# A fused transformer block on one core: key tile in three blocks, value tile with its own history, and a new written-out order

## The chip, the core and the metric

The kernel runs on one core of a Trainium2 chip. A core has five engines with their own instruction streams: TensorE (PE in the profile; its weight loads are listed apart as PEld), VectorE (DVE), ScalarE (ACT), GpSimd (POOL) and SyncE (SP). SP issues nearly all transfers here; they run on the core's 16 DMA engines. The engines meet only through semaphores: an instruction waits until what it reads has been written. Each engine works through its own list in the order in which the program issued it, so an instruction that waits holds up everything behind it on its engine. The metric is the time of one execution in microseconds (us); it was measured three times for the kernel before.

## The reference

One block of a transformer on x of 2048 rows by 512, in bf16. A vector c gives, through SiLU and w_mod, six vectors of 512: shift, scale and gate for each half.

```
mod = silu(c) @ w_mod                      # six vectors sa, ca, ga, sb, cb, gb
h = layernorm(x) * (1 + ca) + sa
q, k, v = h @ wqkv                         # 32 heads of 16
# position s looks at s, s-2, ..., s-14 (8 places, none before 0)
attn = softmax(q[s] . k[s - 2w] / 4 over w)
x = x + ga * ((sum over w of attn * v[s - 2w]) @ wo)
h = layernorm(x) * (1 + cb) + sb
x = x + gb * ((gelu(h @ w_gate) * (h @ w_up)) @ w_down)
```

The hidden width of the last part is 1792.

## The kernel before, in words

The rows are worked on in four groups of 512 (`sg` 0 to 3). A group passes through these steps, each a Python generator that yields `Op` objects; an `Op` has an engine, the names that must be done before (`after`), buffer slots that it takes and gives, and a function that issues the instructions.

- Norm 1 (`LN1.sg`): statistics on DVE (`st0` to `st3`, line 430; one or more of the four are done on ACT, `sa` and `sq`, lines 408 and 419), then the reciprocal root on POOL (`rs0`, line 471), then the scaling on DVE (`x0` to `x3`, line 448) into the tile xn. POOL's `rs0` reads what DVE wrote (`vd0`, `va0`, lines 460 and 465), and `x0` reads what POOL wrote.
- Turning the normed rows (`transp`): for group 0 and 1 by TensorE (`LN1.0.th`, line 509; `LN1.1.t0`, `t1`, line 484), for groups 2 and 3 by a transposing transfer that SP issues (`LN1.2.t`, `LN1.3.t`, line 490).
- Scale and shift (`h0` to `h3`, one for each 128 columns): group 0 on DVE and ACT out of PSUM, groups 1 and 3 on ACT (line 527), group 2 on POOL (line 525). They write hT, which the projection reads.
- Projection (`qp.sg.blk.j`, four matmuls of 512 columns each, line 598): blk 0 is q, 1 is k, 2 is v; j is one of four sets of heads. A matmul of index dt reads h of the same index. ACT empties PSUM (`qkv.sg.blk.j`).
- Logits: DVE multiplies q with eight shifted views of k (`pq.sg.j`, line 664, one instruction of 128x4096), TensorE sums with a small matrix in 32-column tiles (`lp`, line 678, eight matmuls that run four at a time).
- Softmax on DVE, with the exponential on ACT (`mx`, `z`, `e`, `s1`, `ri`, `p`), then the weights are turned (`ptp` on TensorE for group 0, a write to DRAM and four reads, `est` and `ptl`, for groups 1 to 3).
- Values: v goes to DRAM (`vst`, line 635) and comes back in four reads, each for 32 partitions and shifted by two rows against the next (`V4.sg.0` to `V4.sg.2` and `V4ld.sg`, line 644). DVE multiplies (`pv.sg.j`, line 771), TensorE sums (`o.sg.j`, line 790).
- Output projection (`x1p`), the addition of x (`x1`), norm 2 (`LN2.sg`), then the gated part: 14 pairs of `g` and `u` (line 844), `gl` and `ub` on ACT, their product `hh` on DVE, the down projection `y` (line 856), the last addition `ot` and the store `sto`.

Gates: the vector ga is made on TensorE (`mp2`), copied (`gc2`), written to DRAM (`gst2`, line 319) and read back to all partitions (`ga`, line 323), where it scales wo (`woS`). The same is done for gb (`mp5`, `gst5`, `gb`).

What runs when is fixed by one list of numbers, `ORDER`: each number names a generator, and its next `Op` is issued. There is no planner at run time, and nothing reorders. The list fixes the order of each engine:

```
for i in ORDER:
    op = nxt[i]
    ...
    op.fn()
```

K lies in one tile with room for three groups and 16 columns of history in front (`kT`, line 170); the view of group sg starts 14 columns before its first. When group 3 writes over group 0, a copy (`halo`, line 630) brings the last columns of group 2 to the front. V has one tile for a group (`v4`, one buffer) that holds the group's 512 positions and 8 before them, so each read fetches rows of 520 elements. A mask tile serves the first positions of group 0.

Of the kernel before, what the change touches and what calls it, by code (L numbers as in the profile page):

```python
# [106 lines left out]
def kernel(  # L107
# [23 lines left out]
    VH = 16  # L131
    VR = S + VH

# [5 lines left out]
    NB = {"x": 4, "hT": 2, "xn": 2, "q": 4, "vs": 1, "v4": 1, "prod": 5, "h2": 2,  # L139
# [17 lines left out]
    maskT = const.tile([H, W, 16], F32, name="maskT")  # L157
# [12 lines left out]
    kT = const.tile([P, 4, 3 * SG + 16], BF16, name="kT")  # L170
# [10 lines left out]
    def setup():  # L181
# [7 lines left out]
        def f1():  # L189
            nc.gpsimd.memset(M[:], 1.0)  # L190
            nc.gpsimd.affine_select(out=M[:], in_=M[:], pattern=[[-4, H]], compare_op=ALU.is_ge, fill=0.0, base=0,
                                    channel_multiplier=1)
            nc.gpsimd.affine_select(out=M[:], in_=M[:], pattern=[[4, H]], compare_op=ALU.is_ge, fill=0.0, base=3,
                                    channel_multiplier=-1)
            nc.gpsimd.memset(maskT[:], 0.0)
            for w in range(1, W):
                nc.gpsimd.memset(maskT[:, W - 1 - w, 0:2 * w], NEG)
        yield Op("POOL", 2.5, f1, fire="consts")

        def f2():  # L200
            nc.gpsimd.memset(kT[:, :, 0:16], 0.0)
# [4 lines left out]
            B["V4", 0] = T("v4", [P, 4, 4, SG + 8], BF16, "V4")  # L206
            for w4 in range(4):
                nc.gpsimd.memset(B["V4", 0][H * w4:H * w4 + H, :, :, 0:8 + 2 * w4].rearrange("p i j s -> p (i j) s"), 0.0)
        yield Op("POOL", 3.0, f2, take=[SL["v4"]], fire="M2", after=["LN1.0.rs2"])
# [11 lines left out]
    def loads():  # L221
# [20 lines left out]
        def ldwm01(b):  # L242
            if "wm01" not in B:
                B["wm01"] = T("prod", [P, 2, 4, D], BF16, "wm01")
            nc.sync.dma_start(out=B["wm01"][:, b, :, :], in_=w_mod[:, b * D:(b + 1) * D].rearrange("(t p) n -> p t n", p=P))

        def ldc():
            nc.scalar.dma_start(out=c4[:], in_=c.rearrange("o (t p) -> (o t) p", p=P))
# [24 lines left out]
        def act_q():  # L273
            yield Op("ACT", 0.46, ldx(0, 2, 4, nc.scalar), fire="x0.2", lat=mb(0.25), dma=True)
            yield Op("ACT", 0.45, ldc, fire="c", lat=0.0, dma=True)
        qs = [act_q()]
# [5 lines left out]
        for b in range(3):  # L282
            qs.append(one("SP", 0.55, ldq(b), fire=f"wqkv{b}", lat=mb(0.5)))
        for g in range(1, NSG):
# [41 lines left out]
    def mods():  # L326
# [15 lines left out]
        for b in (1, 0):  # L342
            def f(b=b):
                if b:
                    B["mp01"] = T("mm", [P, 8], F32, "modT_ps")
                for ch in range(4):
                    for kt in range(4):
                        nc.tensor.matmul(B["mp01"][:, 4 * b + ch:4 * b + ch + 1],  # L348
                                         lhsT=B["wm01"][:, b, kt, ch * P:(ch + 1) * P], rhs=scT[:, kt:kt + 1],
                                         start=(kt == 0), stop=(kt == 3))  # L350
            yield Op("PE", 0.43, f, after=[f"wm{b}", "scT", "w15"], take=[SL["mm"]] if b else [],
                     give=[] if b else [SL["prod"]], fire=f"mp{b}")
# [3 lines left out]
        yield Op("DVE", 0.1, f, after=["mp0", "ident"], give=[SL["mm"]], fire="mod01")  # L356
# [137 lines left out]
    PART = ((0, (0, 1), False), (0, (2, 3), True), (1, (0,), False), (1, (1, 2, 3), True))  # L494

# [3 lines left out]

    def transp0(key, ev):  # L500
        for half in range(2):
            def f(half=half):
                for hf, dts, onv in PART:
                    if hf == half:
                        ps = T("mm", [P, len(dts), 256], BF16, "hTp") if half else T("att", [P, 2, SG], BF16, "hTp")
                        B[key, half, onv] = ps
                        for n, dt in enumerate(dts):
# [25 lines left out]
    def transp0_ev(key, dkey, sc, bi, ev, dep, eng):  # L533
        for half, dts, onv in PART:
            if onv != eng:
                continue
# [441 lines left out]
```

## Time and profile before

| what | value |
|---|---|
| time of three runs | 236.9 us median, 236.7 to 237.16 |
| profiled execution, first to last instruction | 234.1 us |
| TensorE busy | 230.0 us |
| VectorE busy | 170.4 us |
| ScalarE busy | 150.0 us |
| GpSimd busy | 18.6 us |
| DMA, all queues | 30.21 MB |

The profile is of one execution. Its own time is known only as its span, 234.1 us from the first instruction to the last; the measured times hold what lies around the span too, so the median of the runs stands 2.8 us above it. Times in a timeline are counted from the start of the span. In a row of a timeline stand the start, the length, the engine (a q behind it marks the engine's sequencer, which issues transfers), the line of the kernel, the instruction, what it writes and reads, and how many were merged; in brackets the idle time of the engine before it and what ended it. The length of a matmul runs to its last result, which is later than the start of the next one: the distance between two starts is what a matmul takes from the stream.

### The profile page before, as it was taken

Reading aid. Unit: us, or ns where it says so; the run is one execution under the profiler, and the core shown is the slowest. Engines: PE = TensorE matmul, PEld = TensorE weight load, DVE = VectorE, ACT = ScalarE, POOL = GpSimd, SP = SyncE. Lnnn points to the kernel's source line nnn. Section 1 sums busy time; section 2 is a strip of 40 time slices with the busy share of each in tenths; the row PEclk is TensorE's granted clock in tenths of the full one; section 3 lists DMA queues with packets and bytes.
Section 4 is the critical chain, followed back from the end, with each engine's and each line's share of the span. In section 5 each row is a group of like instructions: output and inputs, shape, how many; then the busy total and the mean of one; then the engine's idle time right before and its main releaser. Section 6 shows DMA issues by size and latency. Waiting matters only on the chain.

```text
span 234.1 us, 3675 instructions
## 1 busy us (share of the span) xinstructions
PE 230.0 (98%) x1387; PEld 108.2 (46%) x1387; DVE 170.4 (73%) x240; ACT 150.0 (64%) x283; POOL 18.6 (8%) x43
## 2 busy tenths in 40 slices
PE   7999999999999999999999999999999999999995
PEld 2755455434644444444444444444444444444443
DVE  3999999999997999999799788467747421222222
ACT  4899997976997758936656492546754343666400
POOL 2612461000100000100000010000001000000000
PEclk9999999999999999999999999999999999999999
DMA  6997989999969839553102963510000411000011
GB/s 218 373 364 213 202 213 171 276 391 303 176 152 236 291 92 200 98 114 103 56 0 57 202 109 60 156 56 0 0 4 0 90 45 45 3 0 0 0 48 45
DMA packets 36265, 30.21 MB, mean 129 GB/s; under 512 B 14872, under 2 KB 34328, under 8 KB 36248
## 3 DMA queue, kind: packets, MB, share of 16 engines
q1 hardware_dynamic: 35968, 29.72, 50.6%
q10 hardware_dynamic: 280, 0.26, 0.3%
q8 instruction: 11, 0.18, 0.3%
q14 instruction: 6, 0.05, 0.1%
HBM read 22.37 MB, written 4.98 MB: 117 GB/s over the span
## 4 chain that ended last, share of the span: by engine, by line
PE 98%; DVE 0%; issue 0%
PE g_ps L844 21%; PE u_ps L844 21%; PE y_ps L856 19%; PE qkv_ps L598 17%; PE x_ps L811 6%; PE o_ps L790 3%; PE LTp L678 3%; PE warm_ps L217 3%; PE y_ps L868 1%; PE qkv_ps L580 1%; PE hTp L484 1%; PE hTp L509 0%; PE modT_ps L305 0%; PE modT_ps L348 0%; PE gR_ps L369 0%; PE PTp L736 0%
## 5 line engine op out<-in xcount | busy, mean ns | idle before, releaser
L844 PE MATMUL g_ps<-h,Wg 128*128 128x512 bf16 x224 | 57.5, 379 | 0.0
L844 PE MATMUL u_ps<-h,Wu 128*128 128x512 bf16 x224 | 57.5, 379 | 0.0
L878 ACT ACTIVATE gl<-g_ps 128x512 bf16<-128x512 f32 x56 | 33.6, 600 | 24.8 <-PE g_ps L844 23.9
L856 PE MATMUL y_ps<-Wd,hht 128*128 128x512 bf16 x210 | 46.0, 379 | 0.0
L885 ACT CAST ub<-u_ps 128x512 bf16<-128x512 f32 x56 | 32.8, 586 | 18.3 <-PE u_ps L844 18.1
L598 PE MATMUL qkv_ps<-hT,wqkv 128*128 128x512 bf16 x184 | 42.1, 380 | 0.0
L896 DVE TENSOR_TENSOR hht<-gl,ub 128x512 bf16<-128x512 bf16 x56 | 23.0, 421 | 25.3 <-ACT ub L885 25.0
L664 DVE TENSOR_TENSOR pq<-qT,kT 128x4096 bf16<-128x4096 bf16 x16 | 36.3, 2292 | 0.0
L771 DVE TENSOR_TENSOR pv<-PT,V 128x4096 bf16<-128x4096 bf16 x16 | 36.0, 2286 | 0.0
L844 PEld LDWEIGHTS <-Wg 128*128 128x128 bf16 x224 | 21.5, 98 | 27.3 <-issue 2.1
L844 PEld LDWEIGHTS <-Wu 128*128 128x128 bf16 x224 | 21.8, 98 | 26.6 <-issue 0.4
L856 PEld LDWEIGHTS <-hht 128*128 128x128 bf16 x210 | 20.5, 98 | 24.8
L598 PEld LDWEIGHTS <-wqkv 128*128 128x128 bf16 x184 | 20.1, 114 | 19.7 <-issue 3.0
L903 DVE TENSOR_TENSOR ot<-y_ps,x 128x512 bf16<-128x512 f32 x15 | 10.3, 689 | 20.2 <-PE y_ps L856 17.2
L471 POOL TENSOR_TENSOR rstd<-rstd,neghalf 128x4 f32<-128x4 f32 (+1 forms) x9 | 8.8, 980 | 154.1 <-DVE rstd L460 85.5
L527 ACT ACTIVATE h<-h,modT,scl 128x512 bf16<-128x512 bf16 x12 | 8.8, 802 | 11.6 <-DMA h<-xn 11.6
L811 PE MATMUL x_ps<-woP,oT 128*128 128x512 bf16 x64 | 15.3, 379 | 0.0
L430 DVE BATCH_NORM_STATS2 st<-x 128x6 f32<-128x512 bf16 x19 | 12.9, 680 | 3.1 <-DMA x<-in_A_x_dram 2.9
L820 DVE TENSOR_TENSOR x<-x_ps,x 128x512 bf16<-128x512 f32 x16 | 10.8, 686 | 5.0 <-PE x_ps L811 5.0
L801 ACT CAST oT<-o_ps 128x512 bf16<-128x512 f32 x16 | 8.9, 592 | 2.7 <-PE o_ps L790 2.7
L618 ACT CAST qT<-qkv_ps 128x512 bf16<-128x512 f32 x16 | 9.2, 587 | 2.2 <-PE qkv_ps L598 2.1
L620 ACT CAST kT<-qkv_ps 128x512 bf16<-128x512 f32 x16 | 9.5, 596 | 1.2 <-PE qkv_ps L598 1.2
(85 smaller groups left out, 181.5 us busy)
## 6 DMA issues: line engine op xcount, KB each, us to landing
V<-vscr SPq DMA_DIRECT2D x12, 520.0 KB, 10.4
wm<-in_w_mod_dram SPq DMA_DIRECT2D x6, 512.0 KB, 5.4
vscr<-vT SPq DMA_DIRECT2D x4, 512.0 KB, 4.2
out_dram<-ot SPq DMA_DIRECT2D x15, 128.0 KB, 1.7
Wg<-in_B_w_gate_dram SPq DMA_DIRECT2D x1, 1792.0 KB, 11.0
Wu<-in_B_w_up_dram SPq DMA_DIRECT2D x1, 1792.0 KB
wqkv<-in_A_wqkv_dram SPq DMA_DIRECT2D x3, 512.0 KB, 8.3
x<-in_A_x_dram SPq DMA_DIRECT2D x3, 512.0 KB, 8.6
```

The costliest lines, as they stand in the source:

```text
L430: nc.vector.bn_stats(out=st[:], in_=src()[:, c4, :])
L598: nc.tensor.matmul(ps[:], lhsT=wqkv[blk][:, dt, j::4], rhs=B["hT", sg][:, :, dt, :], start=(dt == 0), stop=(dt == DT - 1))
L664: nc.vector.tensor_tensor(out=pq[:], in0=_ap(B["qT", sg][:, j, :], [[0, W], [1, SG]]), in1=_ap(kT[:, j, sg % 3 * SG + 2:sg % 3 * SG + 2 + ...
L771: nc.vector.tensor_tensor(out=t[:], in0=_ap(B["PT", sg][:, 0, :], [[SG, 2], [0, 4], [1, SG]]), in1=_ap(v[:, 0, j, :], [[8, 2], [4 * (SG + ...
L811: nc.tensor.matmul(ps[:], lhsT=B["oT", sg][:, j, c4::CPS] if sg else B["oT", sg][:, j, c4 * P:(c4 + 1) * P], rhs=woP[:, j, :], start=(j == ...
L820: nc.vector.tensor_tensor(out=x[:, c4, :], in0=B["x1ps", sg, c4][:], in1=x[:, c4, :], op=ALU.add)
L844: nc.tensor.matmul(ps[:], lhsT=Wt[:, dt, ft * P:(ft + 1) * P], rhs=B["h2T", sg][:, :, dt, :], start=(dt == 0), stop=(dt == DT - 1))
L856: nc.tensor.matmul(ps[:], lhsT=B["hh", sg, ft][:, c4 * P:(c4 + 1) * P], rhs=B["Wd", ft // 4][:, ft % 4, :], start=(ft == 0), stop=(ft == F ...
L878: nc.scalar.activation(out=gl[:], in_=B["g", sg, ft][:], func=ACT.Gelu_apprx_tanh)
L885: nc.scalar.copy(out=ub[:], in_=B["u", sg, ft][:])
L896: nc.vector.tensor_tensor(out=hh[:], in0=B["gl", sg, ft][:], in1=B["ub", sg, ft][:], op=ALU.mult)
L903: nc.vector.tensor_tensor(out=ot[:], in0=B["y", sg, c4][:], in1=B["x", sg][:, c4, :], op=ALU.add)
```

## The change

K gets three blocks, each with 16 columns of history of its own. For groups 1 to 3 a copy on ACT (`kh.sg`) fills the history from the block before; `halo` goes. The mask lies in the third K block until group 2 writes there. V becomes one tile whose rows have 16 columns of history and 512 of the group. Each of the four reads now fetches rows of 512 elements (1024 bytes); the eight older positions come by a copy on POOL inside the tile (`vh.sg`), which waits for the last multiplication of the group before (`pv`), and the reads wait for this copy. Zeros in front of v in DRAM are written by a transfer of their own (`vz`).

At the start, w_mod's first two blocks come in four loads by rows and not in two by columns, wqkv's first block in two loads, c is loaded from POOL's queue and not from ACT's, and the first loads are issued in one fixed sequence. The first two vectors are summed load by load (`mp01.0` to `mp01.3`). The turning of group 0 goes by quarters, and three and not two parts of q are begun on half a group. There are 15 filler matmuls on zeros before the first work and not 20.

All engines get a new order. Where the text needs it (names as above; `|` marks nothing but a pause for the eye):

```
VectorE before: ... LN1.1.st0 st1 st2 vd0 va0 | LN1.2.st0 st1 | pq.0.0 | LN1.2.st2 vd0 va0 | LN1.1.x0-x3 |
   LN1.2.x0-x3 | pq.0.1 pq.0.2 pq.0.3 pq.1.0 | lm.0 mx.0 z.0 | pq.1.1 | s1.0 LN1.3.x0-x3 ri.0 p.0 | pq.1.2 | pv.0.0-3
VectorE after:  ... LN1.1.st0 st1 st2 vd0 va0 | LN1.1.x0-x3 | pq.0.0 pq.0.1 pq.0.2 | LN1.2.st0 st1 st2 vd0 va0 |
   pq.0.3 | LN1.2.x0-x3 | lm.0 mx.0 z.0 | pq.1.0 | s1.0 ri.0 p.0 LN1.3.x0-x3 | pq.1.1 | pv.0.0-3
TensorE before: ... LN1.1.t0 qp.0.1.3 LN1.1.t1 mp2 mp3 lp.0.0 | six qp.1 | lp.0.1 lp.0.2 lp.0 | five qp.1 | qp.2.0.0
   qp.1.1.3 | five qp.2 | ptp.0 lp.1.0 | four qp.2 | lp.1.1 o.0.0 lp.1.2 | qp.2.0.3 o.0.1 qp.2.1.3 o.0.2 qp.3.0.0
TensorE after:  ... LN1.1.t0 t1 qp.0.2.3 lp.0.0 qp.0.1.3 lp.0.1 mp3 | three qp.1 | lp.0.2 | two qp.1 | lp.0 | two qp.1 |
   mp5 qp.1.1.1 mp2 | four qp.1 | qp.2.0.0 qp.2.1.0 qp.2.2.0 ptp.0 qp.2.2.1 qp.2.2.2 lp.1.0 qp.2.2.3 qp.2.0.1 lp.1.1
   qp.2.1.1 o.0.0 o.0.1 qp.3.0.0
SyncE before:   ... vst.0 LN1.2.t V4.0.0 gst2 V4.0.1 ga vst.1 V4.0.2 V4ld.0 LN1.3.t vst.2 wm4 Wg Wu V4.1.0 ...
SyncE after:    ... vst.0 wm5 wo1 V4.0.0 V4.0.1 LN1.2.t vst.1 V4.0.2 V4ld.0 gst2 ga LN1.3.t gst5 vst.2 wm4 Wg V4.1.0 Wu ...
GpSimd before:  ident consts LN1.0.rs0 rs2 M2 LN1.1.rs0 LN1.2.rs0 LN1.2.h0-h3 LN1.3.rs0 LN2.0.rs0 ...
GpSimd after:   c ident LN1.0.rs0 rs2 consts M2 LN1.1.rs0 LN1.2.rs0 LN1.2.h0-h3 LN1.3.rs0 vh.1 LN2.0.rs0 vh.2 ...
```

The core of the diff:

```diff
 ORDER = [
-    23, 23, 23, 23, 23, 23, 23, 23, 23, 23, 23, 2, 0, 0, 23, 1, 1, 22, 2, 31, 31, 31, 33, 22, 23, 22, 33, 33,
...
+    19, 19, 19, 19, 19, 19, 19, 19, 19, 19, 19, 3, 2, 29, 29, 0, 1, 3, 18, 29, 29, 3, 3, 3, 3, 3, 3, 27, 27, 27,
...
-    VH = 16
+    VH = 64
     VR = S + VH
+    VW = SG + 16
...
-    maskT = const.tile([H, W, 16], F32, name="maskT")
...
-    kT = const.tile([P, 4, 3 * SG + 16], BF16, name="kT")
+    kT = const.tile([P, 4, 3, SG + 16], BF16, name="kT")
+    maskT = kT[0:H, 0, 2, 16:16 + 16 * W].rearrange("p (w s) -> p w s", s=16)
+    V4 = const.tile([P, 4, 4, VW], BF16, name="V4")
...
-            for b in (1, 0):
-                yield Op("SP", 0.5, lambda b=b: ldwm01(b), take=[SL["prod"]] if b else [], fire=f"wm{b}", lat=mb(0.5))
+            for kt in range(4):
+                yield Op("SP", 0.5, lambda kt=kt: ldwm01(kt), take=[] if kt else [SL["prod"]], fire=f"wm01.{kt}", lat=0.635)
+            for a in range(2):
+                yield Op("SP", 0.5, ld(wqkv[0][:, 2 * a:2 * a + 2, :], wq_v[:, 2 * a:2 * a + 2, 0:D]), fire=f"wqkv0.{a}", lat=mb(0.25))
...
-    def halo():
-        yield Op("ACT", 0.25, lambda: nc.scalar.copy(out=kT[:, :, 0:16], in_=kT[:, :, 3 * SG:3 * SG + 16]),
-                 after=[f"qkv.2.1.{j}" for j in range(4)] + [f"pq.0.{j}" for j in range(4)], fire="halo")
+    def khalo(sg):
+        if sg:
+            yield Op("ACT", 0.25, lambda: nc.scalar.copy(out=kT[:, :, sg % 3, 0:16], in_=kT[:, :, (sg - 1) % 3, SG:SG + 16]),
+                     after=[f"qkv.{sg - 1}.1.{j}" for j in range(4)] + [f"pq.0.{j}" for j in range(4) if sg == 3], fire=f"kh.{sg}")
+    def vzero():
+        yield Op("SP", 0.6, lambda: nc.sync.dma_start(out=vscr[:, :, VH - 16:VH], in_=gB[:, 0:64].rearrange("p (j s) -> p j s", j=4)), after=["warm"],
+                 fire="vz", lat=1.2)
...
+    def vhist(sg):
+        if sg:
+            def f():
+                nc.gpsimd.tensor_copy(out=V4[:, :, :, 8:16].rearrange("p i j s -> p (i j) s"),
+                                      in_=V4[:, :, :, VW - 8:VW].rearrange("p i j s -> p (i j) s"))
+            yield Op("POOL", 0.5, f, after=[f"pv.{sg - 1}.3"], fire=f"vh.{sg}")
+    def vread(sg):
         for w4 in range(4):
             def f(w4=w4):
-                if w4 == 0 and sg:
-                    B["V4", sg] = T("v4", [P, 4, 4, SG + 8], BF16, "V4")
-                z = 0 if sg else 8 + 2 * w4
-                src = bass.AP(vscr.tensor, vscr.offset + VH + sg * SG - 8 - 2 * w4 + z,
-                              [[16 * VR, H], [VR, 16], [1, SG + 8 - z]])
...
+                src = bass.AP(vscr.tensor, vscr.offset + VH + sg * SG - 2 * w4, [[16 * VR, H], [VR, 16], [1, SG]])
+                nc.sync.dma_start(out=V4[H * w4:H * w4 + H, :, :, 16:VW].rearrange("p i j s -> p (i j) s"), in_=src)
...
-    pl.spawn(warmup(13, 20))
+    pl.spawn(warmup(13, 15))
```

More of the change, by code (lines that the diff above doesn't have):

```diff
@@ L194, in f1 @@
                                     channel_multiplier=-1)
-            nc.gpsimd.memset(maskT[:], 0.0)
+            nc.gpsimd.memset(maskT, 0.0)
             for w in range(1, W):
@@ L205, in f2 @@
                                         base=-H * w4, channel_multiplier=1)
[L206 to L209, printed above, removed]
+            nc.gpsimd.memset(V4[:, :, :, 0:16].rearrange("p i j s -> p (i j) s"), 0.0)
+        yield Op("POOL", 2.2, f2, fire="M2", after=["LN1.0.rs2"])
     def warmup(cold, n):
@@ L340, in mods, with f @@
                  act="exp", fire="pre")
-        for b in (1, 0):
-            def f(b=b):
-                if b:
+        for kt in range(4):
+            def f(kt=kt):
+                if kt == 0:
                     B["mp01"] = T("mm", [P, 8], F32, "modT_ps")
[L346 to L352, printed above, removed]
+                for ch in range(8):
+                    nc.tensor.matmul(B["mp01"][:, ch:ch + 1], lhsT=B["wm01"][:, kt, ch * P:(ch + 1) * P],
+                                     rhs=scT[:, kt:kt + 1], start=(kt == 0 and ch == 0), stop=(kt == 3 and ch == 7))
+            yield Op("PE", 0.23, f, after=[f"wm01.{kt}", "scT"], take=[] if kt else [SL["mm"]],
+                     give=[SL["prod"]] if kt == 3 else [], fire=f"mp01.{kt}")
         def f():
             nc.vector.tensor_tensor(out=mod01[:], in0=B["mp01"][:], in1=c01[:], op=ALU.add)
-        yield Op("DVE", 0.1, f, after=["mp0", "ident"], give=[SL["mm"]], fire="mod01")
+        yield Op("DVE", 0.1, f, after=["mp01.3", "ident"], give=[SL["mm"]], fire="mod01")
     def mods_g(k):
@@ L570, with mm, f @@
     QKV = [(0, 0), (1, 0), (2, 0), (2, 1), (2, 2), (2, 3), (0, 1), (1, 1), (0, 2), (1, 2), (0, 3), (1, 3)]
-    QKV0 = [(0, 0), (0, 1), (0, 2), (1, 0), (1, 1), (0, 3), (1, 2), (2, 0), (2, 1), (2, 2), (2, 3), (1, 3)]
+    QKV0 = [(0, 0), (0, 1), (0, 2), (0, 3), (1, 0), (1, 1), (1, 2), (2, 0), (2, 1), (2, 2), (2, 3), (1, 3)]
     def qkv_halves():
-        for half in range(2):
-            for n, dt in enumerate(((2, 0, 3, 1), (0, 1, 2, 3))[half]):
-                def f(half=half, n=n, dt=dt):
-                    for j in range(2):
-                        if half == 0 and n == 0:
-                            B["qkvps", 0, 0, j] = T("mm", [P, SG], F32, "qkv_ps")
-                        nc.tensor.matmul(B["qkvps", 0, 0, j][:, half * 256:half * 256 + 256],
-                                         lhsT=wqkv[0][:, dt, j::4], rhs=B["hT", 0][:, 2 * half:2 * half + 2, dt, :],
-                                         start=(n == 0), stop=(n == DT - 1))
-                yield Op("PE", 0.218, f, after=[f"LN1.0.h{dt}.{half}", "wqkv0"],
-                         take=[SL["mm"]] * 2 + [SL["q"]] if half == 0 and n == 0 else [], fire=f"qph.{half}.{dt}")
-        for j in range(2):
-            pl.done[f"qp.0.0.{j}"] = pl.done["qph.1.3"]
+        def mm(half, j, dt, n):
+            nc.tensor.matmul(B["qkvps", 0, 0, j][:, half * 256:half * 256 + 256], lhsT=wqkv[0][:, dt, j::4],
+                             rhs=B["hT", 0][:, 2 * half:2 * half + 2, dt, :], start=(n == 0), stop=(n == DT - 1))
+        for dt in range(DT):
+            def f(dt=dt):
+                for j in range(3):
+                    if dt == 0:
+                        B["qkvps", 0, 0, j] = T("mm", [P, SG], F32, "qkv_ps")
+                    mm(0, j, dt, dt)
+            yield Op("PE", 0.328, f, after=[f"LN1.0.h{dt}.0", f"wqkv0.{dt // 2}"],
+                     take=[SL["mm"]] * 3 + [SL["q"]] if dt == 0 else [], fire=f"qph.{dt}")
+        for j in range(3):
+            def f(j=j):
+                for dt in range(DT):
+                    mm(1, j, dt, dt)
+            yield Op("PE", 0.437, f, after=[f"LN1.0.h{dt}.1" for dt in range(DT)], fire=f"qp.0.0.{j}")
     def qkv(sg):
@@ L601, in qkv @@
             tk = {0: [SL["q"]], 1: [], 2: [SL["vs"]]}[blk] if j == 0 else []
-            yield Op("PE", 0.856, f, after=[f"LN1.{sg}.h{d}" for d in (("0.1", "1.0", "3.1") if sg == 0 else (2, 3))] + [f"wqkv{blk}"], take=[SL["mm"]] + tk,
+            yield Op("PE", 0.856, f, after=[f"LN1.{sg}.h{d}" for d in (("2.1", "3.1") if sg == 0 else (2, 3))] + ([f"wqkv{blk}"] if blk else []), take=[SL["mm"]] + tk,
                      give=[SL["hT"]] if last else [], fire=f"qp.{sg}.{blk}.{j}")
@@ L619, in g @@
                 elif blk == 1:
-                    nc.scalar.copy(out=in_rows(kT[:, j, 16 + sg % 3 * SG:16 + (sg % 3 + 1) * SG], sg), in_=by_rows(ps, sg))
+                    nc.scalar.copy(out=in_rows(kT[:, j, sg % 3, 16:16 + SG], sg), in_=by_rows(ps, sg))
                 else:
@@ L689, in f @@
                 L = B["LT", 0][0:H, :, 0:16]
-                nc.vector.tensor_tensor(out=L, in0=L, in1=maskT[:], op=ALU.add)
+                nc.vector.tensor_tensor(out=L, in0=L, in1=maskT, op=ALU.add)
             yield Op("DVE", 0.32, f, after=["lp.0", "consts"], fire="lm.0")
```

106 lines of the change are left out of this document (55 added, 51 removed), and 68 rows, old and new, of the table ORDER.

## The prediction

> **What bounds the kernel now.** I read the page first: busy shares, slices and the chain that ended last.
>
> ```profile
> span 234.1 us, 3675 instructions
> ...
> PE 230.0 (98%) x1387; PEld 108.2 (46%) x1387; DVE 170.4 (73%) x240; ACT 150.0 (64%) x283; POOL 18.6 (8%) x43
> ...
> PE   7999999999999999999999999999999999999995
> ...
> DVE  3999999999997999999799788467747421222222
> ...
> PEclk9999999999999999999999999999999999999999
> ...
> GB/s 218 373 364 213 202 213 171 276 391 303 176 152 236 291 92 200 98 114 103 56 0 57 202 109 60 156 56 0 0 4 0 90 45 45 3 0 0 0 48 45
> ...
> PE 98%; DVE 0%; issue 0%
> ```
>
> TensorE is the chain. A busy PE need not stream at its peak, so next the chain in order of time (start, length) and PE's timeline.
>
> ```profile
> 141.25 12.09 PE y_ps L856 x56
> ...
> 228.23 3.07 PE y_ps L868 x28
> ```
>
> ```profile
> 1.25 4.88 PE L217 MATMUL warm_ps<-gB 128*128 128x512 bf16 x11 [1.25 <-DVE gB L212]
> ...
> 9.26 0.81 PE L217 MATMUL warm_ps<-gB 128*128 128x512 bf16 x3
> 9.91 2.02 PE L580 MATMUL qkv_ps<-hT,wqkv 128*128 128x256 bf16 x16
> ...
> 22.75 5.40 PE L598 MATMUL qkv_ps<-hT,wqkv 128*128 128x512 bf16 x24
> 28.08 1.48 PE L678 MATMUL LTp<-pq,Mph 128*32 128x512 bf16 x24
> 29.49 10.55 PE L598 MATMUL qkv_ps<-hT,wqkv 128*128 128x512 bf16 x48
> 39.97 0.62 PE L736 MATMUL PTp<-e,ident 128*32 128x256 bf16 x16
> ```
>
> 56 matmuls in 12.09 us are 0.216 us each, and 48 from 29.49 to 39.97 are 0.218: the same rate early and late. No engine keeps TensorE waiting from the first projection at 9.91 to the last matmul at 228.23 + 3.07 = 231.30. So there are two things to win or lose: when that stream begins, and what is put into it, work or waits. VectorE is nearly full up to about 95 us (the slices); its order decides whether TensorE's is met.
>
> **The head.** Rows of VectorE in the head and behind it:
>
> ```profile
> 8.34 0.41 DVE L448 TENSOR_SCALAR xn<-x,sums,rstd 128x512 bf16<-128x512 bf16 x1
> 8.78 0.17 DVE L355 TENSOR_TENSOR mod<-modT_ps,c 128x8 f32<-128x8 f32 x1
> 8.98 1.68 DVE L543 TENSOR_SCALAR hT<-hTp,mod 128x256 bf16<-128x256 bf16 x5
> 10.58 0.69 DVE L430 BATCH_NORM_STATS2 st<-x 128x6 f32<-128x512 bf16 x1
> ...
> 13.19 0.14 DVE L465 TENSOR_SCALAR rstd<-sums 128x1 f32<-128x1 f32 x1
> ...
> 20.56 0.41 DVE L448 TENSOR_SCALAR xn<-x,sums,rstd 128x512 bf16<-128x512 bf16 x1
> 20.88 8.89 DVE L664 TENSOR_TENSOR pq<-qT,kT 128x4096 bf16<-128x4096 bf16 x4
> 29.69 0.28 DVE L690 TENSOR_TENSOR LTp<-LTp,maskT 32x128 f32<-32x128 f32 x1
> ```
>
> Now the first scaled hT begins at 8.98, because `mod01` waits for all its matmuls, and three fillers stand before the first projection. After the change `mod01` comes before the last xn, so hT begins at about 8.8, and its first piece (1.68/5 = 0.33, plus its tail) is written by 9.2; the sixteen turned squares are the same, and the fillers between are gone. I take 9.2 as the start: 0.71 earlier. Bounds: 9.91, if c from POOL's queue or the four loads come late (c's reader on ACT had to wait even now), and 9.0, if nothing does. Two matmuls of 256 columns replace one of 512, which by 0.216 a row of 512 is no difference. Later VectorE steps gain less, 0.2 us, since the same instructions stand before 10.58: I take 10.4.
>
> **Tile runs.** Entering and leaving the 32-column instructions costs. From 28.08 to 29.49 are 1.41 us for 24 that run four at a time, 6 x 0.216 = 1.30, so 0.11 on one side; from 22.75 to 28.08 are 5.33 for 24 x 0.216 = 5.18, so 0.15 around. I take 0.21 a run, 0.11 to 0.26. The new order has 17 runs and not 15: +0.44 (0.2 to 0.5).
>
> **The first wait: projection of group 2.** Rows of POOL and of SP, ACT's after a transposing transfer, and the DMA issues from 30.8 to 33 (KB, us to landing):
>
> ```profile
> 13.49 1.02 POOL L471 TENSOR_TENSOR rstd<-rstd,neghalf 128x4 f32<-128x4 f32 x1 [3.12 <-DVE rstd L465]
> 18.30 1.25 POOL L471 TENSOR_TENSOR rstd<-rstd,neghalf 128x4 f32<-128x4 f32 x1 [3.79 <-DVE rstd L465]
> 26.62 6.05 POOL L525 TENSOR_SCALAR hT<-hT,mod 128x512 bf16<-128x512 bf16 x4 [7.07 <-ACT gl L408]
> ```
>
> ```profile
> 21.09 3.42 SPq L490 DMA_TRANSPOSE hT<-xn  x1
> 24.61 0.62 SPq L644 DMA_DIRECT2D V<-vscr  x1
> 25.32 0.61 SPq L319 DMA_DIRECT2D gscr<-gR  x1
> ...
> 30.42 0.38 SPq L323 DMA_DIRECT2D gB<-gscr  x1
> 30.90 0.59 SPq L635 DMA_DIRECT2D vscr<-vT  x1
> 31.54 1.72 SPq L644 DMA_DIRECT2D V<-vscr  x2
> ...
> 99.75 2.02 SPq L490 DMA_TRANSPOSE h<-xn  x1
> ```
>
> ```profile
> 104.23 2.93 ACT L527 ACTIVATE h<-h,modT,scl 128x512 bf16<-128x512 bf16 x4 [2.36 <-DMA h<-xn]
> ```
>
> ```profile
> vscr<-vT SPq DMA_DIRECT2D x1, 512.0 KB, 4.5
> V<-vscr SPq DMA_DIRECT2D x1, 508.0 KB, 7.3
> V<-vscr SPq DMA_DIRECT2D x1, 506.0 KB, 9.2
> ```
>
> Now xn of group 2 is finished at 20.56 + 0.41 = 20.97, POOL begins 5.65 later, and the projection of group 2 follows at 33.84 (five of the twelve fours behind 29.49). The change puts xn of group 2 behind all four `pq.0`. VectorE, added up: from 10.4 the norm takes 13.33 - 10.58 = 2.75, to 13.15. Then `LN1.1.x0` stands directly behind `va0`, with nothing between: POOL starts 0.16 later (13.49 - 13.33) and takes 1.02, so VectorE idles to 14.4, which other work filled before. Four xn at 0.32: 15.7. Three `pq` at 2.20 ((29.69 - 20.88)/4): 22.3. The norm of group 2 again 2.6: 24.9. `pq.0.3`: 27.1. If POOL's root for group 2 runs under `pq.0.3`, xn is written by 28.5; if it must wait for its end, by 29.5.
>
> Which? POOL's four h took 6.05, of which 29.69 - 26.62 = 3.07 lay under `pq`, and what is left, 2.98, is four times 0.75, what an undisturbed h takes. So POOL got nothing done under `pq`, for a 128x512 operand. I take the later end, 29.5, and keep 28.5 for the range.
>
> [...]
>
> From xn to h: 5.65 us at 20.97, 4.5 from issue at an idle queue (104.23 - 99.75). With reads of V in flight I take 5.0: POOL begins at 34.5 and is through h3 at 37.5. TensorE's date: before it was at 33.84; the new list has, ahead of it, one qp more (+0.86), `mp5` (+0.22), three more runs (+0.63), and starts 0.71 earlier: 34.8, and its fourth matmul, which reads h3, at 35.45. It waits 2.05 us (0.5 to 3.1).
>
> **The second wait: projection of group 3.** SP holds the transposing transfer 2.0 to 3.4 us; 2.7 from 29.6 is 32.3. Then come `vst.1`, two V reads, `gst2`, and `ga`, which waits until `gst2` has landed. Before, `gst2` landed only with the V read ahead of it (`ga` at 30.42), and now both remaining reads are ahead of it. From issue of `vst.1` (30.90) to landing of the second read (32.2 + 9.2 = 41.4) are 10.5 us. The reads become rows of 1024 bytes: no faster at worst; at best 520 KB at the best slices' 373 GB/s, 1.4 us and not 2.56 (41.4 - 38.84), twice: 8.2. I take the middle, 9.35: 41.65, `ga` 0.4, so group 3's transposing transfer is issued at 42.1, where xn of group 3 stands ready by 39.3. Before, it was at 37.46. h0 starts 4.5 later, four h in 2.93 with one copy between them (0.4): h3 at 49.9. TensorE without waits reaches group 3 after eight qp (6.9), five tile groups (2.2) and four runs (0.84): 44.7, and its fourth matmul at 45.4, where before it came only at 49.01. All waits together are 4.5; the second adds 2.45 to the first.
>
> **What costs nothing, and its cover.** The `kh` copies (nearest: a PSUM copy, 0.6 us, three for one) stand on ACT before h of group 3, where ACT waits anyway. `vh` on POOL is 0.2 to 0.8 by the rows above, but can be held back by `woS` and a `pq` until about 54; `V4.1.0` waits for it, and now the load Wu behind it on SP. V and Wu, 2.3 MB at 365 GB/s, are there by about 63; the first u comes at 70. `vz`, the split loads and the smaller memset of V add four SP issues of 0.6, before 20 us, where SP has idle time. The mask is read by 30, before K's third block is written. Behind group 3's projection VectorE has 2 to 4 us in hand, as TensorE is late; output banks are held longer by `ot.0.3` and `ot.1`, which I cost at nothing, up to 1.5.
>
> **The sum.** -0.71 + 0.44 + 4.5 = +4.2 us. The profiled span would be 238.3, and on the median of the runs, 2.8 above the span, 236.9 + 4.2 = **241.1 us**. Lower end of these costs: root not held (-1.05), SP held 2.0 (-0.7), reads 8.2 (-1.15): +1.3, 238.2. Upper: +0.7, +1.15, transposing 5.65 (+1.15): +7.2, 244.1.
>
> **The rivals.**
> - *All in time.* TensorE never waits: -0.27, 236.6; with tile runs at 0.11 each, -0.49, 236.4. One mechanism would do it: with the shorter V rows the rings stand free and both transposing transfers land early. The point is h0 of group 2 by 32.4, under 3 us after xn at 29.5, and of group 3 by 42.1. Against it stand 4.5 and 5.65. Chance 0.14: 0.08 no change, 0.06 faster.
> - *Only the first wait.* `gst2` doesn't queue behind the V reads and group 3's transfer starts at 39.4: h3 at 47.2, covered by the first wait. +1.8, 238.7; with the root not held 237.6. Against it: `ga` at 30.42. Chance 0.15.
> - *The clock falls in a wait.* At the start a matmul takes 4.88/11 = 0.44 us, twice the later rate, for 4.9 us: a relapse costs about 2.4, 243.5. [...] Chance 0.05. [...]
> - *Later banks.* The held banks add 1.5: 242.6. Before, `ot.0.3` was issued soon behind its sum. Chance 0.06.
> - The forecast itself: 0.60.
>
> **How the numbers follow.** 0.2% of 236.9 is 0.47 us, about what a measurement of this kernel can tell from no change. Slower: 0.60 + 0.15 + 0.05 + 0.06 = 0.86; same 0.08; faster 0.06. The range leaves out the first rival and the last ends of the forecast: 237.4 to 243.6.
>
> **What would show it.** In the profile after: the first 256-column projection at about 9.2; VectorE idle 1.2 us ahead of group 1's xn, waiting for POOL; POOL's root of group 2 twice as long; an idle TensorE of some 2 us at about 35 before group 2 and again at 46 to 50 before group 3, with POOL and ACT behind the transposing transfers; `ga` late by ten us; then 0.216 a matmul to the end. I am wrong if TensorE streams through 34 to 50 without a gap, or loses its time after 65.

## The result, and the profile after

The changed kernel takes 250.8 us in the median (249.3 to 251.8) beside 236.8 for the kernel before: a ratio of 1.058 (95% interval 1.054 to 1.062). The prediction was slower, 241.1, at most 243.6. Direction and the first two waits are as predicted; nearly two thirds of the loss are somewhere else. Executions more than 1.5% above the fastest of their kernel are left out below: two of the four of new_order_old_parts (255.7 and 256.5 us) and one of est1_ahead (254.4).

Rows of the changed kernel's page (the execution of 251.76 us):

```profile
span 250.0 us, 3668 instructions
...
PE 233.7 (93%) x1373; PEld 108.1 (43%) x1386; DVE 170.1 (68%) x240; ACT 149.9 (60%) x285; POOL 23.4 (9%) x44
...
PE   8999978889999798999799999969999999999995
...
PEclk9999999999999999999999999997999999999999
...
PE 42%; DVE 28%; DMA 16%; issue 4%; SPq 4%; POOL 3%; ACT 2%; DVEq 0%; POOLq 0%
```

VectorE's work is what it was (170.1 us beside 170.4), and TensorE has nearly the same instructions (1386 weight loads beside 1387). The chain that ended last was TensorE to 98% and is now TensorE, VectorE and transfers by turns: the engines wait for each other. A table by stage of the same kernel shows where (stretch, its length, busy time of TensorE, weight loads, VectorE, ScalarE, GpSimd with their instructions, granted clock, DMA share, GB/s):

```profile
34.00:40.00 6.00, 3.75 (x16) 1.65 (x15) 4.03 (x6) 2.58 (x7) 4.01 (x5) 1.00 1.09 268
...
48.00:52.00 4.00, 2.30 (x14) 0.89 (x14) 4.00 (x2) 4.00 (x7) 0.00 (x0) 1.00 0.21 69
52.00:71.00 19.00, 18.95 (x137) 9.68 (x136) 17.03 (x23) 15.63 (x33) 4.36 (x2) 1.00 1.05 307
71.00:82.00 11.00, 11.00 (x53) 4.99 (x52) 7.49 (x6) 8.80 (x15) 0.00 (x0) 1.00 0.65 130
82.00:94.00 12.00, 9.73 (x85) 3.84 (x83) 11.71 (x9) 4.79 (x9) 0.00 (x0) 1.00 0.46 151
...
118.00:126.00 8.00, 6.69 (x29) 2.83 (x29) 5.70 (x5) 6.53 (x11) 0.00 (x0) 1.00 0.52 148
...
163.00:169.00 6.00, 3.91 (x41) 1.45 (x39) 6.00 (x4) 2.53 (x4) 0.00 (x0) 1.00 0.46 87
169.00:174.00 5.00, 5.00 (x19) 1.93 (x16) 2.34 (x5) 3.40 (x7) 0.00 (x0) 0.66 0.31 105
```

A lone matmul is shown as 0.38 us long where a row of them takes 0.216 each, so idle time understates a loss. Counted from one weight load to the next against 0.216 a matmul of 512 columns, the new losses are 15.7 us: 6.0 up to 65 us (the projection), 3.1 from there to 97 (gated layer of group 0), 2.5 to 140 (group 1) and 4.1 to 174 (group 2). With 0.41 gained at the first projection (9.50) and an estimate of 0.44 for two more runs of 32-column products that is within 0.2 of the difference of the spans, 15.9. Not all of the 4.1 is waiting: in the last row of the table the clock is granted at 0.66, and in a finer stretch at 0.50 from 169.6 to 173.0. Four matmuls there are 1.71 us from start to start (170.49 to 172.20), four later ones 0.86 (174.34 to 175.20). Half of the 3.4 us, 1.7, is an estimate of the most that TensorE loses by it.

The two waits that the prediction worked out, on GpSimd (a row of the chain), SyncE and TensorE:

```profile
25.32 3.00 POOL rstd L474
...
29.75 3.68 SPq L493 DMA_TRANSPOSE hT<-xn  x1
...
43.05 0.37 SPq L328 DMA_DIRECT2D gB<-gscr  x1
43.53 3.02 SPq L493 DMA_TRANSPOSE hT<-xn  x1
...
36.72 0.38 PE L609 MATMUL qkv_ps<-hT,wqkv 128*128 128x512 bf16 x1 [1.11 <-POOL hT L533]
...
48.84 0.38 PE L609 MATMUL qkv_ps<-hT,wqkv 128*128 128x512 bf16 x1 [0.23 <-ACT hT L535]
...
50.73 0.38 PE L609 MATMUL qkv_ps<-hT,wqkv 128*128 128x512 bf16 x1 [0.81 <-ACT hT L535]
```

And those that it left out, behind 65 us. TensorE waits for V products of VectorE, and VectorE for the probabilities (`PT`) and for V; the kernel before has none of the three (engine that waits, what for, us in total, times, longest):

```profile
PE o_ps L809 <- DVE pv L789: 5.6, 6, 1.7
...
DVE pv L789 <- DMA PT<-escr: 5.1, 2, 3.8
DVE pv L789 <- DMA V<-vscr: 4.3, 1, 4.3
```

### The profile page after: what moved, and what is told of

The parts are those of the page before. It is cut to its first block, busy times and chain, and to the rows that moved or that the text cites. A ratio compares the mean times of both kernels' runs of the same rounds, so it can differ in the third digit from the quotient of the medians.

```text
span 250.0 us, 3668 instructions
## 1 busy us (share of the span) xinstructions
PE 233.7 (93%) x1373; PEld 108.1 (43%) x1386; DVE 170.1 (68%) x240; ACT 149.9 (60%) x285; POOL 23.4 (9%) x44
## 4 chain that ended last, share of the span: by engine, by line
PE 42%; DVE 28%; DMA 16%; issue 4%; SPq 4%; POOL 3%; ACT 2%; DVEq 0%; POOLq 0%
PE u_ps L863 12%; PE g_ps L863 11%; PE y_ps L875 10%; DVE pv L789 9%; DMA escr<-e 6%; DVE pq L683 4%; DMA hT<-xn 4%; PE x_ps L830 4%; PE qkv_ps L609 3%; DVE xn L451 3%; SPq L777 2%; DVE st L433 2%; DMA V<-vscr 2%; DMA PT<-escr 2%; POOL rstd L474 2%
## 5 line engine op out<-in xcount | busy, mean ns | idle before, releaser
L863 PE MATMUL g_ps<-h,Wg 128*128 128x512 bf16 x224 | 58.3, 382 | 1.3 <-ACT gl L897 0.7
L863 PE MATMUL u_ps<-h,Wu 128*128 128x512 bf16 x224 | 58.4, 384 | 0.0
L609 PE MATMUL qkv_ps<-hT,wqkv 128*128 128x512 bf16 x180 | 43.4, 380 | 4.1 <-POOL hT L533 2.2
L609 PEld LDWEIGHTS <-wqkv 128*128 128x128 bf16 x180 | 19.3, 114 | 24.4 <-issue 9.2
L474 POOL TENSOR_TENSOR rstd<-rstd,neghalf 128x4 f32<-128x4 f32 (+1 forms) x9 | 10.7, 1188 | 90.8 <-DVE rstd L463 56.2
L809 PE MATMUL o_ps<-pv,Msum 128*32 128x512 bf16 x128 | 9.5, 383 | 5.7 <-DVE pv L789 5.6
L656 POOL COPY V<-V 128x128 bf16<-128x128 bf16 x3 | 5.6, 1873 | 71.3 <-DVE pv L789 71.3
```

The source lines that it names most:

```text
L474: nc.gpsimd.tensor_tensor(out=k["rstd"][:, a:b], in0=k["rstd"][:, a:b], in1=neghalf[:, a:b], op=ALU.pow)
L609: nc.tensor.matmul(ps[:], lhsT=wqkv[blk][:, dt, j::4], rhs=B["hT", sg][:, :, dt, :], start=(dt == 0), stop=(dt == DT - 1))
L863: nc.tensor.matmul(ps[:], lhsT=Wt[:, dt, ft * P:(ft + 1) * P], rhs=B["h2T", sg][:, :, dt, :], start=(dt == 0), stop=(dt == DT - 1))
```

## The experiments

Orders below are lists of operation names on one engine, as in the description of the kernel. "Old order" is the order of the kernel before, "new" that of the change.

**Order or data parts?** Two kernels separate them.

```diff
 new_order_old_parts: the kernel before
-  all engines behind the first projection: old order
+  all engines behind the first projection: new order
 old_order_new_parts: the changed kernel
-  all engines behind the first projection: new order
+  all engines behind the first projection: old order
```

> The kernel before with its own data parts and its own head, but with all five engines in the new order behind the first projection. Theory 1 (the order costs it): 248 to 252 us, with TensorE waits at the projections of groups 2 and 3 and in the later stages as in the changed kernel. Theory 2 (the data parts cost it): under 242 us.

> All data parts of the change (K in three blocks with history copies, V in rows of 1024 bytes with its history copy on GpSimd, head loads in the new sequence, 15 warm-ups, scale and shift by rows, first projection in thirds) in the engine orders of the kernel before, from the first projection on. Theory 1, the order of the engines costs the 14 us and the data parts nearly nothing: 236.8 - 0.4 (the head as measured) + 0.4 (two more 32-column tile runs) = 236 to 238 us. Theory 2, the data parts cost it (history copy on GpSimd, rows of 1024 bytes that land later): 241 us or more, with the waits for V and for the probabilities still in the trace.

The new order in the old kernel takes 251.7 and 252.4 us, a ratio of 252.0 / 236.6 = 1.065, with waits at the projections of groups 2 and 3 and in all three later stages: it costs the whole loss without any of the new data parts. But the new parts in the old order are not at 237 either: 242.7, ratio 1.026 (1.024 to 1.027). All of that is lost before 55 us, none behind. VectorE's groups between 12 and 56 us in that run, with what ended their idle time:

```profile
L677 DVE TENSOR_TENSOR pq<-qT,kT 128x4096 bf16<-128x4096 bf16 x7 | 16.2, 2344 | 4.9 <-ACT kT L635 4.9
...
L427 DVE BATCH_NORM_STATS2 st<-x 128x6 f32<-128x512 bf16 x5 | 3.4, 672 | 1.4 <-DMA x<-in_A_x_dram 1.4
```

Two causes, then. The second row is the input of group 2, loaded behind `wqkv2` now; the old order wants it early. The first row is the wait for a K history copy (`kh`, L635). The multiplies that wait read only columns of their own block, and the copy writes the margin of another block; but the blocks lie in one tile, and the multiplies stand behind the copy in program order. I removed them one after the other.

```diff
 old_order_x2_first: old_order_new_parts
-  SyncE: x1 wqkv1 wqkv2 x2
+  SyncE: x1 wqkv1 x2 wqkv2
 old_order_three_k_tiles: old_order_x2_first
-    kT = const.tile([P, 4, 3, SG + 16], BF16, name="kT")
+    kT = [const.tile([P, 4, SG + 16], BF16, name=f"kT{b}") for b in range(3)]
...
```

> All data parts of the change in the engine orders of the kernel before, as in old_order_new_parts (242.7 us), with one transfer moved: the input of group 2 is loaded ahead of the third block of the projection weights, as before, instead of behind it. Theory: the 6 us of that run come from the input of group 2 landing at 14.7 us instead of 13.0, which the old VectorE order waits for ahead of group 1 (1.4 us there, and every multiply behind it 4 us later); with it early again the data parts cost nothing: 236 to 237 us, and under 236.5 if the head's 0.4 us is kept. Rival: the rows of 1024 bytes or the history copies hold the old order up as well: 239 us or more.

> As old_order_x2_first (241.0 us: all data parts of the change, old order, input of group 2 early), with one change: the three K blocks are three tiles instead of one. In that run VectorE waited 4.9 us for the K history copies ahead of multiplies that do not read them (2.5 us ahead of the second K multiply of group 0, 2.4 us ahead of the third of group 1); those multiplies are issued behind the copy and read the same tile. Theory: that wait is what the data parts cost in the old order; with three tiles it goes, and the time is 241.0 - 4.9 = 236 to 237 us. Rival: the V rows of 1024 bytes or the V history copy on GpSimd cost too and take its place: 239 us or more.

The first gave 1.7 us (241.0, ratio 1.017, 1.015 to 1.020) and not 6: of its theory only the 1.4 us of the row above held. The second gave the other 4.8: 236.26 us, ratio 0.9976 (0.9961 to 0.9991). This is faster than both kernels, than the one before by only 0.24%. TensorE's waits in it, whole span:

```profile
PE warm_ps L211 <- DVE gB L206: 1.2, 1, 1.2
PE modT_ps L346 <- ACT scT L336: 0.8, 1, 0.8
PE scp L332 <- ACT s L327: 0.3, 1, 0.3
```

and the chain:

```profile
PE 93%; ACT 3%; DMA 2%; issue 1%; DVE 0%; POOLq 0%
```

So K in blocks, V rows of 1024 bytes and both history copies cost nothing that can be measured, as soon as the copies don't tie other blocks down. The new order costs 250.8 - 236.3 = 14.5 us. (In the changed kernel itself no K multiply waits for a copy: its order places them.)

**Which stages?** Spliced orders, all with the changed kernel's parts; "from" is a cut on every engine.

```diff
 new_then_old_order:     new order | from g.0.0: old order
 old_then_new_order:     old order | from g.0.0: new order
 old_from_third_layer:   new order | from y.1.0.0: old order
 sync_new_rest_old:      as new_then_old_order, SyncE new to the end
```

> The changed kernel, but from the first matmul of the gated layer of group 0 on every engine goes back to the old order; the projection stage stays in the new one. If each wait is its own loss: the two waits of the projection stage stay (2.9 and 2.5 us) and the 10 us behind it go: 236.8 + 5.7 = 242 to 243 us. If the early waits are the cause of the late ones: 248 us or more. If the early waits are made good later: 237 to 238 us.

> The changed kernel, but with the old order up to the first matmul of the gated layer of group 0, and the new order from there on; the load and product of the last modulation part stay at their old place, since the old first half has not made them. If each wait is its own loss: the 10 us of the later stages stay, 245 to 248 us. If they follow from the lateness of the projection stage: 237 to 240 us.

> The changed kernel, but from the down projection of group 1 on every engine goes back to the old order (transpose of group 2 ahead of the probabilities of group 3, V products of group 3 on TensorE behind eight gate and up pairs instead of ahead of them). Theory: each stage's loss is its own; the 3.9 us of TensorE waits ahead of and in the gated layer of group 2 go, all waits ahead of it stay: 250.8 - 3.9 = 246.9 us (246 to 248). Rival: they are passed on from the stages ahead and come back at another place: 250 to 251 us.

> As new_then_old_order (242.9 us: new order up to the gated layer of group 0, old order behind it), but SyncE keeps the new order to the end; TensorE, ScalarE and VectorE have the old one from the gated layer on. If the place of the transfers (last V reads behind the probabilities or ahead of them, stores) is what costs the 8 us of the later stages: 247 to 251 us. If it is the place of the products on TensorE and of the work on VectorE, which ask for the same transfers 3 to 10 us earlier: 243 to 244 us.

Measured: 242.9 (ratio 1.027, 1.024 to 1.030), 254.0 (1.074, 1.070 to 1.078), 248.1 (1.047, 1.044 to 1.050) and 254.4 (1.072, 1.069 to 1.076). Read as a ledger from the fastest kernel: projection stage 242.9 - 236.3 = 6.6; gated layers of groups 0 and 1, 248.1 - 242.9 = 5.3; layer of group 2, 250.8 - 248.1 = 2.7. In new_then_old_order and old_from_third_layer the part in old order has next to no waits (0.0 and 0.3 us), whatever came before: a late start isn't handed on. In old_then_new_order the new second half costs 254.0 - 242.7 = 11.3, more than the 7.9 in the changed kernel, so the stages are not wholly independent. The clock blurs the borders of this ledger: all four executions of new_then_old_order have a mean granted clock of 0.993. At 0.50, as in the changed kernel, that is 3.4 us of its span of 242.2 (an estimate from the mean), which costs up to 1.7. In the changed kernel's profile the 3.4 us stand at 169.6, behind the projection stage; sync_new_rest_old, in the same order up to the gated layer of group 0, has 0.59 from 51 to 55. Up to 1.7 of the 6.6 may thus be clock and not waiting.

The last of the four fits neither of its expectations. TensorE streams through the layers of groups 0 and 1 although SyncE keeps the new order; then it stands still once:

```profile
PE g_ps L857 <- ACT h L529: 6.9, 1, 6.9
```

SyncE's rows there (start, length):

```profile
154.56 0.33 SPq L763 DMA_DIRECT2D escr<-e  x1
156.60 1.88 SPq L771 DMA_DIRECT2D PT<-escr  x3
158.52 0.60 SPq L941 DMA_DIRECT2D out_dram<-ot  x1
159.16 0.56 SPq L771 DMA_DIRECT2D PT<-escr  x1
159.76 0.61 SPq L658 DMA_DIRECT2D V<-vscr  x1
160.49 4.46 SPq L487 DMA_TRANSPOSE h<-xn  x1
```

The new SyncE order puts the transposing transfer of group 2 behind the probabilities of group 3, which the old VectorE order makes after the normalisation that feeds that transfer. One engine's order is neither good nor bad alone; what hurts is an order that asks a partner for something it makes later.

**Single waits.** Four kernels each move one thing in the changed kernel.

```diff
 group2_ahead
-  VectorE: pq.0.1 pq.0.2 LN1.2.st0..va0 pq.0.3 LN1.2.x0..x3      TensorE: lp.0 qp.1.2.3 qp.1.0.1
+  VectorE: pq.0.1 LN1.2.st0..va0 pq.0.2 LN1.2.x0..x3 pq.0.3      TensorE: qp.1.2.3 qp.1.0.1 lp.0
 group3_ahead
-  SyncE: V4ld.0 gst2 ga LN1.3.t
+  SyncE: V4ld.0 LN1.3.t gst2 ga
 est1_ahead
-  SyncE: V4.1.2 V4ld.1 est.1 ptl.1.0
+  SyncE: V4.1.2 est.1 V4ld.1 ptl.1.0
 v4ld3_ahead
-  SyncE: V4.3.2 est.3 ptl.3.0 .. pt.3.1 V4ld.3 LN2.2.t
+  SyncE: V4.3.2 V4ld.3 est.3 ptl.3.0 .. pt.3.1 LN2.2.t
```

> The changed kernel, but VectorE normalises group 2 before its last two K multiplies of group 0 (statistics ahead of the third, the four writes ahead of the fourth), and TensorE takes the last logit product of group 0 two projections later. Theory: the wait at the projection of group 2 comes from xn of group 2 standing behind those multiplies; it shrinks from 2.9 to under 0.5 us, the waits behind it stay: 250.8 - 2.5 = 248.3 us. Rival, the later waits have their own clock (VectorE or the V reads): the wait goes, but a later one grows by as much, 250 to 251 us.

> The changed kernel, with one transfer moved: SyncE issues the transposing transfer of group 3 ahead of the store and the read back of the first gate. Theory: SyncE no longer waits for that store, the transpose starts when xn of group 3 is written (41.3 us) and the wait at the projection of group 3 falls from 2.5 to about 0.4 us: 250.8 - 2 = 248.8 us. Rival: the transpose is held by the V reads in the rings whatever its place, no change, 250.8 us.

> The changed kernel, with one transfer moved: the store of the probabilities of group 1 is issued ahead of the last V read of group 1, as in the kernel before. Theory: the store lands some 2 us after its issue instead of 6.5, the first V multiply of group 1 starts at 78 to 79 us instead of 82.3, and TensorE's waits in the gated layer of group 0 (3.4 us) go to under 1: 250.8 - 2.5 = 248.3 us. Rival: the rings are full with the gate and up weights anyway, and the store or the V read that now stands behind it lands as late: 250.8 us.

> The changed kernel, with one transfer moved: the last V read of group 3 is issued ahead of the probabilities of group 3 instead of behind them. Theory: it lands by 152 us, the first V multiply of group 3 starts at about 156 us (when the probabilities have landed) instead of 159.0, the normalised group 2 and its transpose follow 3 us earlier, and TensorE's waits ahead of the gated layer of group 2 fall from 3.9 to about 1 us: 250.8 - 2.9 = 248 us. Rival: the probabilities then land later by as much, since they queue behind that read: 250.8 us.

None gained what its theory said: 252.3, 251.9, 249.8 and 250.3 us, beside 250.8. In group2_ahead xn of group 2 was written 2.3 us earlier (27.4), and the transfer landed at 36.0 all the same, beside 35.7: SyncE held it 4.97 us, not 3.68, behind the V reads issued before it.

```profile
24.80 1.31 SPq L658 DMA_DIRECT2D V<-vscr  x2
27.45 4.97 SPq L487 DMA_TRANSPOSE hT<-xn  x1
```

It is even slower: its two executions with a mean clock of 1.00 took 252.2 and 252.4 us, those of the changed kernel 249.3 and 250.2. The move brought new waits ahead of 34 us (ScalarE's K history copy 1.6 us behind a K multiply, TensorE 1.3 us for ScalarE's `qT`); no run separates which of them costs the 2 us.

In group3_ahead the wait at the projection of group 3 did go (the transfer was issued at 41.78, not 43.53), and the first V multiply of group 1 then waited 5.0 us for its probabilities, not 3.8: it has its own date, 82.3 in the changed kernel and 83.2 here. At a mean clock of 1.00 its one execution took 249.6, between the 249.3 and 250.2 of the changed kernel. In est1_ahead the store landed 2.6 us after its issue, that VectorE wait fell to 0.57, and TensorE's waits in the layer of group 0 from 3.1 to 0.4. Its executions took 248.9 to 250.7 us, beside 249.3 to 251.8: the ranges overlap. The two profiled executions, both at a mean clock of 0.993, differ by 2.0. So a gain of 1 to 2 us is possible, and the theory's 2.5 is neither shown nor refuted. In v4ld3_ahead the rival is shown: the store of the probabilities, behind one more V read, took 153.57 - 148.01 = 5.6 us to its reader and not 2.9, and the V multiply started at 158.63 (158.98 in the changed kernel):

```profile
158.63 2.29 DVE L783 TENSOR_TENSOR pv<-PT,V 128x4096 bf16<-128x4096 bf16 x1 [3.83 <-DMA PT<-escr]
```

**Two gates?** At group 2, gate a is VectorE's order, gate b the place of the transfer behind two V reads. Both kernels stand on new_then_old_order with three K tiles.

```diff
 group2_gate_b
-  SyncE: V4.0.0 V4.0.1 LN1.2.t
+  SyncE: LN1.2.t V4.0.0 V4.0.1
 group2_gates_ab
+  also the VectorE and TensorE moves of group2_ahead
```

> As new_then_old_order (242.9 us) with the three K blocks as three tiles and one transfer moved: the transposing transfer of group 2 is issued ahead of the first two V reads of group 0 (gate b); VectorE's order stays. Two gates: the transfer still waits for xn, written at 29.7 us, lands at about 33.5 instead of 35.7, and the V reads start 6 us later; the wait at the projection of group 2 falls from 2.9 to about 1 us, but the first V multiply of group 0 then waits for V, so that 242 to 244 us remain. If the place on SyncE is the only gate: 240 us.

> As group2_gate_b, and VectorE normalises group 2 ahead of the last two K multiplies of group 0, as in group2_ahead (gate a). Two gates: xn is written by 27.4 us, the transfer lands at about 32 us, and the wait of 2.9 us at the projection of group 2 goes; 242.9 - 2.9 = 240 us if the V reads, which start at 31 us instead of 25, are still in time for the first V multiply; if they are not (they land at about 46 us, 2 to 3 us after VectorE asks), the gain is given back at the projection of group 3 or at the V products and 242 to 243 us remain.

Both are slower than the 242.9 they start from: 247.6 (ratio 1.045, 1.041 to 1.049) and 246.0 (1.038, 1.033 to 1.042). The transfer landed at 34.1 and 32.4 us, earlier as expected, but the V reads queue behind it, and V is late at its multiply by 4.9 and 2.6 us; the price of that was undersized. Part of it is the clock's: its mean is 0.979 and 0.986 in all their executions, beside 0.993 in those of new_then_old_order. At 0.50 that is 10.3, 6.8 and 3.4 us (estimates from these means and the spans of 245.8, 244.5 and 242.2), which makes up to 3.5 of the 4.7 us and up to 1.7 of the 3.1 us between them. In the second, VectorE between 20 and 60 us:

```profile
L783 DVE TENSOR_TENSOR pv<-PT,V 128x4096 bf16<-128x4096 bf16 x4 | 8.9, 2288 | 2.6 <-DMA V<-vscr 2.6
```

The old order has neither loss, because it writes xn of group 2 by 21 us: its transfer goes first and V still reads in time. Rows of old_order_three_k_tiles:

```profile
21.45 3.00 SPq L487 DMA_TRANSPOSE hT<-xn  x1
24.67 0.64 SPq L658 DMA_DIRECT2D V<-vscr  x1
```

## Why the prediction was right or wrong

- **Head start, 0.71: half right.** The first projection starts at 9.50, not 9.2; `c` comes late enough that TensorE waits for the sigmoid-weighted input (`scT`) 0.5 us. The bound of 9.91 held. Next to nothing of the gain is left in old_order_three_k_tiles: its first weight load comes at 9.62 beside 9.70 before, and the transposes of group 1 then wait 0.45.
- **Tile runs, +0.44:** nothing contradicts it. The ledger closes with it, which is no measurement of it.
- **First wait, 2.05 (0.5 to 3.1): right, 2.9.** VectorE's dates held to 0.3 us (xn written at 29.72 for 29.5). GpSimd's root was held under the K multiply: 2.99 us long, where that of the group before took 1.03. It ended at 28.31, 0.87 behind the end of that multiply (25.16 to 27.44). The delay lies inside the instruction and not in a wait ahead of it: here engines do not meet only through semaphores. From xn to h were 6.2 us, not 5.0, and the h themselves came later. The wait is 0.85 longer than forecast, inside its range. What I did not see is the second gate: V reads ahead of the transfer set nearly the same date.
- **Second wait, +2.45: right, 2.5.** The mechanism is in the trace: `ga` was issued at 43.05 (forecast 41.65), the transfer right behind it at 43.53 (42.1). That the size fits so well is partly luck: the transfer came 1.4 late, and the first wait had already put TensorE back by 0.85 more than forecast. group3_ahead shows that SyncE's place is its cause, and that the kernel gets nothing for removing it alone.
- **GpSimd's V copy held to about 54: nearly right** (52.47 to 55.83, 3.35 us for a copy that takes 0.37 in group 3), with Wu behind it on SyncE. That V would be "there by about 63" was wrong: the last read of group 1 landed at 77.1. The sum of 2.3 MB holds Wu (1792 KB) and one of the group's four reads (512 KB each); all of them are 3.8 MB. That last read stood ahead of the store of group 1's probabilities, which then took 6.5 us to land.
- **"Behind group 3's projection VectorE has 2 to 4 us in hand ... which I cost at nothing, up to 1.5": the step that failed.** The stretch behind 65 us loses 9.7 us, of which up to 1.7 (the estimate above) is the lower clock; a loss there is what the prediction had named as a sign that it is wrong. VectorE's time in hand went into waits and did not suffice: at its V products it waited 5.1 us for probabilities and 4.3 for V, and TensorE 5.6 for these products. I had worked the order through to 50 us only and let one sentence stand for 120 us of it. In that stretch the new order asks for the first V product of group 1 one and a half gate and up pairs earlier, for those of group 3 eight, and sends the probabilities through queues that hold V reads and weights; the splices put 5.3 and 2.7 us on it in the time.
- **Data parts at nothing: right in sum** (236.3 beside 237.0), by a road I had not seen: multiplies of other blocks of their tile waited 4.9 us for the K copies in old_order_new_parts, and none did in the changed kernel's order or with three tiles.
- **The rival "clock falls in a wait": it happened**, though in the profiled execution not in the two waits priced but at 169 us (0.66 over 5 us), with no idle row longer than 1.7 us. Its price there is at most 1.7 by the estimate above (half of 3.4 us), not 2.4. The slow matmuls at the start (0.44 us each), from which the 2.4 was taken, show no lower clock: it stands at 1.00 from 1.25 to 6.20 in the kernel before. For an output bank TensorE waited 0.7 us in all, behind `gl`.

What stays open: how much of the waits in the layers of groups 0 and 1 is TensorE's early asking and how much late transfers. Of the engines' orders there only SyncE's was swapped alone, and alone it costs nothing in these layers.

## What to carry to other kernels

A written order for five engines must be priced to its end: follow each stage's inputs (here probabilities, V and the transposed norm) through every queue up to the last group, since a stage left out can cost more than those worked out. When a wait has two gates opening within a microsecond, moving one instruction may gain nothing, as here, and may close a third; splice whole stages of a known good order first to find where time is lost, then move single instructions. And when a big rewrite is slower, try its data parts in the old order: here they are worth 0.24%, hidden under 14 us.

## What the runs showed of the hardware that was not expected

- **The clock fell without one long pause.** In the changed kernel it was granted in full through the wait at 36 us (largest gap 1.11) and fell to 0.66 from 169 to 174, after 3.91 busy us of 6 with a largest gap of 1.58. Nearly the same wait at group 3, with gaps of 0.23 to 0.81 in the changed kernel and 0.33 to 0.81 in est1_ahead, left the clock at 1.00 in the first profile and took it to 0.66 from 51 to 56 in the second:

```profile
47.00:51.00 4.00, 2.27 (x21) 0.70 (x20) 4.00 (x3) 2.78 (x5) 0.00 (x0) 1.00 0.19 42
51.00:56.00 5.00, 4.67 (x14) 1.69 (x13) 4.75 (x3) 3.74 (x8) 1.15 (x1) 0.66 0.90 281
```

  The thirteen matmuls from 51.69 on took 4.49 us there, the same thirteen in the changed kernel 2.97 (from 51.44): 1.52 more. In sync_new_rest_old, around its pause of 6.93 us, the clock is 0.78 from 161 to 167 and 0.52 from 167 to 175, and eight matmuls are 3.42 us from start to start (170.55 to 173.97), 0.43 each. In the mean clock the 3.4 us of the changed kernel are 0.007 (1.7 / 250), which is the 0.993 of its profile. The scatter of the changed kernel goes with it: its executions at a mean clock of 1.00 took 249.3 and 250.2 us, those at 0.986 and 0.993 took 251.4 and 251.8. The gaps before these two falls were short, with work between them, and nearly the same gaps stand before a fall in one execution and not in another. What makes the clock fall no run shows.
- **How long a transposing transfer held SyncE went with what had been issued before it.** At group 2 it was 1.89 us with the store of v issued 6.3 us before and no V read (group2_gates_ab), 3.00 with that store issued 1.4 us before (old_order_three_k_tiles; such a store lands after 3.6 to 4.2 us in the changed kernel), and 3.68 and 4.97 behind two V reads (the changed kernel, group2_ahead).
- **A wait between regions that don't overlap**: 4.9 us of VectorE for a ScalarE copy into another block of the same tile, gone when each block is a tile (0.0 at the same multiplies in old_order_three_k_tiles). The row names that copy as what ended the wait.
- **Time outside the span is 1.7 to 1.9 us in the executions with the new data parts and 2.2 in those of the kernel before.** Of the 0.7 us that old_order_three_k_tiles wins, more than half lies there. Which part does it wasn't tried. (The 2.8 us that stood between span and median ahead of the prediction compared two different executions.)
